# Exponentials and a power on GpSimd, an earlier table load and another recorded order in an S5 scan with a gated MLP

## The chip, the cores and the metric

The kernel runs on one core of a Trainium2 chip. The metric is device time in microseconds of one launch, the median of three runs; lower is better. Engines are written as in the profile: PE (TensorE), DVE (VectorE), ACT (ScalarE), POOL (GpSimd) and SP (SyncE, which here only issues transfers).

## The reference, cut to what matters

The input x has 2048 positions of 448 channels. It is normalized, and the normalized xn goes two ways: through a diagonal complex recurrence with 448 states (an S5 layer), and through a second normalization and an MLP with 1792 hidden units. The result is x + s * silu(m).

```
xn = layernorm(x)                                   # x: 2048 x 448
dt = exp(log_dt); Lam_bar = exp(dt * Lam)
B_bar = ((Lam_bar - 1) / Lam)[:, None] * Bmat
h_t = Lam_bar * h_(t-1) + B_bar @ xn_t              # 448 complex states
s = 2 * real(Cmat @ h_t) + xn * Dskip
m = gelu(layernorm(xn) @ w1 + b1) @ w2 + b2
out = x + s * silu(m)
```

Only exp(dt * Re Lam) is needed as an exponential beside dt itself; the angles go through sines.

## The kernel before, in words

The 2048 positions are worked on in four groups of 512, each of two blocks of 128 partitions with two positions on a partition. For a group, `ln` normalizes, transfers transpose the result to the layout that PE wants (`xn2T` for the MLP, `xnT` for the scan), `mm1_run` multiplies by w1 (L801), ACT applies GELU out of PSUM (L805), `mm2` multiplies by w2 (L828), and DVE adds b2 to each of its four results (L831), in two PSUM banks (5 and 6) by turns. `bu` multiplies by B (L729), `ssm` runs the scan on DVE, `ym` multiplies by C (L871, L874) and joins the two ways. `m0` makes products of C and B once (L712, L697); they need the seven matrices CQ, which DVE makes from C (L659, L661) and from the factors that `parameters` works out on columns of four numbers.

Group 0 is treated apart. Its two blocks come as separate loads; `first_stats` takes the statistics (L431, L432) and the factor (var + eps)^(-1/2) of the two normalizations in one: on ACT, as Ln and Exp (L434, L435 for block 0, L438, L439 for block 1). `first_apply` scales (L453), PE transposes (L460), and copies bring it back from PSUM (L417). `mm1_run` then works block 0 alone, the last two pairs of hidden units with both blocks, and block 1, over three pairs of PSUM banks; each pair has to be emptied by GELU before it is used again. A product of w1 is split in two phases, and the second needs a copy of a part of w1 (L352).

`parameters` turns rows to columns on PE (L529, L530), copies them (L532), and then forms dt = exp(log_dt) on ACT (L533), the angles (L534 to L540), exp(dt * Re Lam) on ACT (L541), the wrapped angles (L542 to L544, and L552), their absolute values on ACT (L554) and the sines (L545 to L551). The rest of it is some thirty products on columns of four (L561, L564, L573, L592).

`b1_columns` turns the rows of b1, which two transfers on POOL bring (L84), into columns (L602, L603, L605). `dummies` gives PE products without use, between the loads; the first 26 run ahead of the parameters.

The order in which the instructions stand on each engine isn't that of the source. Every operation is recorded as a task with what it reads and writes; a list of task numbers (`ORDER`) is the order of issue, and `SECOND` names the tasks that take the second of two engines given for them (POOL or DVE for `small`, ACT or DVE for copies). Semaphore waits follow from the tasks' reads and writes. A tuple of steps (`STEPS`) sets the order of the source after group 0.

Normalization factors of later groups, and of group 0's first normalization, come from `ln_scale` (L478 to L488): on POOL with a power (L480), on DVE with a Newton iteration, as `SECOND` says.

```
def small(fn, reads=(), writes=(), chain=False):
    kb.either(("pool", fn), ("dve", fn), reads, writes, chain=chain)
...
for k in SECOND:
    self.tasks[k].choose(1)
order = [self.tasks[k] for k in ORDER]
```

Of the kernel before, what the change touches and what calls it, by code (L numbers as in the profile page):

```python
# [10 lines left out]
F32 = dt.float32  # L11
# [148 lines left out]


ORDER = [int(k) for k in """
# [17 lines left out]
""".split()]  # L180
SECOND = [int(k) for k in """
45 53 54 61 63 66 69 74 76 83 112 130 133 158 160 162 163 165 177 184 185 187 189 190 220 222 224 226 228 230 238 248 249 258 266 268 331 362 364 365
384 400 401 436 447 468 480 482 487 491 499 501 502 504 510 528 529 609 612 627
""".split()]


# [14 lines left out]
def bass_recurrent_scan__ssm_conv_s5__mixer_channel_mlp__prompt_kernel(  # L201
# [18 lines left out]
    with ExitStack() as es:  # L220
# [2 lines left out]

        ident = SB("ident", [128, 128])
        mhalf = SB("mhalf", [128, 1, 1], F32)
        dk = SB("dk", [128, 3, NK + 2], F32)
        iota = dk[:, 0, 0:NK]
        sgn = SB("sgn", [128, 4], F32)
# [76 lines left out]
        with nc.Block():  # L305
# [18 lines left out]
            pool(lambda e: e.memset(M0[:, 3, :], 0.0), [], ["M0p"], 0.3, S0 + 1)  # L324
            pool(lambda e: e.memset(h_sb[:, :, :, 0:2], 0.0), [], ["hp0", "hp1"], 0.2, S0 + 1)
            pool(lambda e: e.memset(mhalf[:], -0.5), [], ["mhalf"], 0.1, S0 + 1)
            pool(lambda e: e.memset(eps[:, 0:1], LN_EPS), [], ["eps"], 0.1, S0)
            pool(lambda e: e.memset(eps[:, 1:2], LN_EPS * LN_EPS), ["eps"], ["eps"], 0.1, S0)

# [94 lines left out]
            def first_stats(b):  # L424

                for par in range(2):
                    q = 2 * par + b
                    var, mean = lnmv[:, 0, q, 1:2], lnmv[:, 0, q, 0:1]
                    r1, key = lnw[:, 0, 2, 1, q:q + 1], xk(0)[par:par + 1] if b == 0 else xk(1)
                    src, dst = x_all[:, b, par, :], xn2_sb[:, b, par * 512:par * 512 + D]  # L430
                    dve(lambda e, q=q, src=src: e.bn_stats(lnst[:, q, :], src), key, [f"st{q}"])  # L431
                    dve(lambda e, q=q: e.bn_aggr(lnmv[:, 0, q, :], lnst[:, q, :]), [f"st{q}"], [f"mv0_{q}"])  # L432
                    if b == 0:
                        kb.add("act", [lambda e, var=var, r1=r1: e.activation(r1, var, ACT.Ln, scale=1.0 + LN_EPS, bias=eps[:, 1:2]),  # L434
                                       lambda e, r1=r1: e.activation(r1, r1, ACT.Exp, scale=-0.5)], [f"mv0_{q}", "eps", "warm"], [f"r1{q}"], chain=True)  # L435
                    elif par == 1:
                        vs2, rs2 = lnmv[:, 0, 1:4:2, 1], lnw[:, 0, 2, 1, 1:4:2]
                        kb.add("act", [lambda e: e.activation(rs2, vs2, ACT.Ln, scale=1.0 + LN_EPS, bias=eps[:, 1:2]),  # L438
                                       lambda e: e.activation(rs2, rs2, ACT.Exp, scale=-0.5)], ["mv0_1", "mv0_3", "eps", "warm"], ["r11", "r13"], chain=True)  # L439

            def gelu_table():
                kb._sem("gelu0")
                kb.add("act", lambda e: e.preload_act_table_set("gelu_apprx_tanh_and_others"), ["cr", "r10", "r12"] + ["r11", "r13"] * (not 0), ["Wg0"], sem="gelu0")

            def first_apply(b):

# [81 lines left out]
            def parameters():  # L528
# [1 line left out]
                   + [lambda e, i=i: e.matmul(psum[64 * i:64 * i + 64, 7, 12:15], vrows[0:3, 448:512], ident[0:3, 0:3], start=True, stop=True) for i in range(2)],  # L530
                   ["vr0", "vr1", "vr2", "ident"], ["ps7"])
                act(lambda e: e.activation(cw[:, 0:3, :], psum[:, 7, 0:16].rearrange("p (t v) -> p v t", v=4)[:, 0:3, :], ACT.Copy), ["ps7"], ["cp"])  # L532
                act(lambda e: e.activation(col(DT), col(LDT), ACT.Exp), ["cp", "warm"], ["cdt"], 0.2, 3 * PINNED - 4, "exp")  # L533
                small(lambda e: e.tensor_scalar(col(F2), col(LIM), 1.0 / TWO_PI, None, op0=ALU.mult), ["cp"], ["f2"])  # L534
                YA, YB, YC, YD = (ang[:, k, :, :, :] for k in range(4))
                A2 = 2 * PINNED
# [1 line left out]
                small(lambda e: e.tensor_scalar(col(F2), ang[:, 0, 0, 0, :], 2.0, None, op0=ALU.mult), ["f1"], ["f2"])  # L538
                small(lambda e: e.tensor_scalar(ang[:, 0, 0, 1, :], ang[:, 0, 0, 0, :], 512.0, None, op0=ALU.mult), ["f1"], ["f3"])
                small(lambda e: e.tensor_tensor(col(A1), col(DT), col(LRE), ALU.mult), ["cdt", "cp"], ["ca"])  # L540
                act(lambda e: e.activation(col(R1), col(A1), ACT.Exp), ["ca"], ["cr"], 0.2, 3 * PINNED - 1, "exp")  # L541
                wrap = [(lambda e: e.tensor_scalar(YB, YA, ROUND, None, op0=ALU.add)),  # L542
                        (lambda e: e.tensor_scalar(YB, YB, ROUND, None, op0=ALU.subtract)),
                        (lambda e: e.tensor_tensor(YA, YA, YB, ALU.subtract))]  # L544
# [366 lines left out]
            def pr(k, g, x=0.0):  # L911
                return P[k] + 10 * g + x

            dummies(26)
            parameters()
            dummies(8, ["vr0"])
            first_stats(0)
# [103 lines left out]
```

## Time and profile before

| | |
|---|---|
| median of three runs | 153.26 us (153.21 to 153.65) |
| profiled execution, span from first to last instruction | 151.8 us |
| the median less the span | 1.5 us |
| PE busy | 147.1 us, 97% |
| DVE busy | 127.6 us, 84% |
| ACT busy | 99.0 us, 65% |
| POOL busy | 42.1 us, 28% |
| granted TensorE clock, mean | 1.000 |

The profile states the profiled execution's time as its span; what lies around the span is known only as the difference to the median. In the page, a busy PE is not a PE at its peak: products overlap, and their ends are modelled. A row of the timeline gives start, length, engine, line, operation, what is written and read, and in brackets the idle time before it with what ended it. The chain that ended last is followed back from the last instruction; its shares show where a stage hangs, and idle time of an engine that isn't in it costs nothing.

### The profile page before, as it was taken

The page shows a single profiled execution, that of the slowest core. Times are in us where ns is not written, and L with a number is a line of the kernel's source. Part 1 is how long each engine was busy: PE and PEld are TensorE (multiplying, and loading weights), DVE is VectorE, ACT ScalarE, POOL GpSimd, SP SyncE. Part 2 cuts the span into 40 slices and gives each one's busy share as a digit, 9 for nine tenths or more (in the row PEclk, how much of TensorE's full clock was granted, in tenths as well). Part 3 has the DMA queues.
Part 4 walks back from the last instruction along what each step waited for, and adds up shares of the span by engine and source line. Part 5 has one row for each costly group of instructions (what it writes and reads, how often), then busy time and mean ns, then how long its engine had stood idle before and what let it go on. Part 6 is the DMA issues. An engine that isn't in the chain of part 4 may idle for free.

```text
span 151.8 us, 2974 instructions
## 1 busy us (share of the span) xinstructions
PE 147.1 (97%) x1127; PEld 86.6 (57%) x1127; DVE 127.6 (84%) x267; ACT 99.0 (65%) x183; POOL 42.1 (28%) x101
## 2 busy tenths in 40 slices
PE   7899999999999999999999999999999999999992
PEld 7785755454566577545444556764454666555551
DVE  2874999999978979999999996379968726999984
ACT  3888996988789559997898610463579834067400
POOL 5376827153020920010456006200072031000201
PEclk9999999999999999999999999999999999999999
DMA  4999999989997300700003032610331001100022
GB/s 116 262 305 390 266 202 138 219 152 133 165 261 180 65 0 0 138 0 4 0 0 63 4 60 45 154 60 4 60 101 23 0 4 57 64 0 0 4 84 98
DMA packets 31236, 14.73 MB, mean 97 GB/s; under 512 B 24752, under 2 KB 30774, under 8 KB 31222
## 3 DMA queue, kind: packets, MB, share of 16 engines
q1 hardware_dynamic: 30912, 14.26, 41.8%
q0 software_dynamic: 160, 0.23, 1.0%
q8 instruction: 9, 0.15, 0.4%
q10 hardware_dynamic: 150, 0.05, 0.1%
q14 instruction: 5, 0.04, 0.1%
HBM read 6.89 MB, written 1.84 MB: 57 GB/s over the span
## 4 chain that ended last, share of the span: by engine, by line
PE 80%; DVE 9%; DMA 4%; SPq 4%; issue 2%
PE psum L828 23%; PE psum L801 22%; PE psum L729 14%; PE psum L871 13%; DMA x_all<-in_A_x_dram 4%; PE psum L874 4%; SPq L84 4%; PE psum L712 3%; DVE xn_sb L499 2%; DVE lnst L399 1%; DVE s_w L628 1%; PE psum L877 1%; DVE o L831 1%; PE psum L697 1%; DVE tmp L891 1%
## 5 line engine op out<-in xcount | busy, mean ns | idle before, releaser
L801 PE MATMUL psum<-xn2T,w_sb 64*128 64x512 bf16 (+1 forms) x462 | 44.6, 345 | 0.3 <-ACT xn2T L417 0.2
L828 PE MATMUL psum<-w_sb,gT 128*128 128x448 bf16 x224 | 44.5, 353 | 0.2 <-DVE o L831 0.2
L805 ACT ACTIVATE gT<-psum,b1f 128x512 bf16<-128x512 f32 (+1 forms) x66 | 35.9, 625 | 10.4 <-PE psum L801 10.2
L801 PEld LDWEIGHTS psum<-xn2T,w_sb 64*128 64x128 bf16 x462 | 24.1, 109 | 19.8 <-ACT gT L805 2.3
L828 PEld LDWEIGHTS psum<-w_sb,gT 128*128 128x128 bf16 x224 | 21.5, 98 | 20.7 <-DVE o L831 0.6
L417 ACT ACTIVATE u_sb<-psum 128x512 bf16<-128x512 f32 (+2 forms) x22 | 10.5, 478 | 23.0 <-PE psum L729 22.7
L729 PE MATMUL psum<-xnT,BT 128*128 128x256 bf16 x196 | 24.0, 273 | 0.0
L729 PEld LDWEIGHTS psum<-xnT,BT 128*128 128x128 bf16 x196 | 18.9, 98 | 5.4 <-issue 1.1
L891 POOL TENSOR_TENSOR tmp<-t,x_all 128x448 bf16<-128x448 bf16 x5 | 5.2, 1032 | 33.1 <-DVE t L888 30.7
L753 DVE TENSOR_TENSOR_SCAN s_w<-dk,vs 128x774 f32<-128x774 f32 x8 | 14.0, 1760 | 0.1
L500 ACT ACTIVATE xn_sb<-x_all,lnw 128x448 bf16<-128x448 bf16 (+2 forms) x21 | 13.0, 662 | 1.2 <-DVE xn_sb L499 1.1
L417 ACT ACTIVATE vs<-s_w 64x256 bf16<-64x256 f32 (+2 forms) x16 | 10.9, 681 | 2.6 <-DVE s_w L753 1.5
L871 PE MATMUL psum<-CZ,h_sb 128*128 128x448 bf16 x56 | 11.9, 352 | 0.0
L871 PE MATMUL psum<-CQ,h_sb 128*128 128x448 bf16 (+2 forms) x54 | 10.5, 332 | 0.0
L399 DVE BATCH_NORM_STATS2 lnst<-x_all 128x6 f32<-128x448 bf16 x12 | 7.1, 617 | 3.4 <-DMA x_all<-in_A_x_dram 3.4
L831 DVE TENSOR_TENSOR o<-psum,b2bc 128x448 f32<-128x448 f32 x16 | 9.7, 614 | 0.2
L871 PEld LDWEIGHTS psum<-CZ,h_sb 128*128 128x128 bf16 x56 | 5.4, 98 | 4.7 <-DVE lnmv L405 0.4
L871 PEld LDWEIGHTS psum<-CQ,h_sb 128*128 128x128 bf16 x54 | 5.1, 98 | 4.0 <-DVE t L885 0.4
L874 PE MATMUL psum<-M,xnT 128*128 128x448 bf16 x32 | 7.4, 352 | 0.0
L480 POOL TENSOR_TENSOR lnw<-lnw,mhalf 128x8 f32<-128x8 f32 x3 | 7.2, 2404 | 0.3
L883 DVE TENSOR_TENSOR Cr<-psum,xd 128x448 f32<-128x448 f32 x7 | 4.3, 620 | 3.5 <-PE psum L877 3.4
L499 DVE TENSOR_SCALAR xn_sb<-x_all,lnw 128x448 bf16<-128x448 bf16 (+2 forms) x19 | 6.9, 396 | 0.0
(160 smaller groups left out, 189.1 us busy)
## 6 DMA issues: line engine op xcount, KB each, us to landing
out_dram<-tmp SPq DMA_DIRECT2D x7, 224.0 KB, 2.0
x_all<-in_A_x_dram SPq DMA_DIRECT2D x3, 448.0 KB, 4.0
w_sb<-in_B_w_dram SPq DMA_DIRECT2D x3, 448.0 KB, 8.4
w_sb<-in_B_w_dram SPq DMA_DIRECT2D x3, 384.0 KB, 4.8
vs<-in_A_C_re_dram SPq DMA_DIRECT2D x1, 392.0 KB, 11.6
Bn<-in_A_B_im_dram SPq DMA_DIRECT2D x1, 336.0 KB, 10.2
Bn<-in_A_B_re_dram SPq DMA_DIRECT2D x1, 336.0 KB, 10.5
vs<-in_A_C_im_dram SPq DMA_DIRECT2D x1, 336.0 KB, 10.8
```

The source lines that it names most:

```text
L399: dve([lambda e, b=b, par=par, q=q: e.bn_stats(lnst[:, q, :], x_all[:, 2 * g + b, par, :])], [f"x{2 * g + b}"] , [f"st{q}"], 0.62, prio)
L417: kb.either(("act", [lambda e, o=o, i=i: e.activation(o, i, ACT.Copy) for o, i in pairs]), ("dve", [lambda e, o=o, i=i: e.tensor_copy(o, i ...
L499: on = [("dve", [lambda e, o=o, i=i: e.tensor_scalar(o, i, rs, nb, op0=ALU.mult, op1=ALU.add) for o, i in parts], 0.4, 0.12), ("act", [lam ...
L500: ("act", [lambda e, o=o, i=i: e.activation(o, i, ACT.Identity, bias=nb, scale=rs) for o, i in parts], 0.75, 0.2)]
L729: fns = [lambda e, r=r, m=m, d=d: e.matmul(psum[:, 4, r * NK:(r + 1) * NK], BT[:, m, d, :], xnT[:, gx, d, :], start=(d == 0), stop=(d == 6 ...
L753: dve(lambda e, so=so, vi=vi: e.tensor_tensor_scan(so, dk[:].rearrange("p i c -> p (i c)"), vi, 0.0, ALU.mult, ALU.add), ["v", "vl", "dk", ...
L801: return lambda e: e.matmul(view(bk[k]), w1_sb[rows, d, fcol(2 * j + k)], rhs[rows, d, :, :], start=not second and n == 0, stop=second and ...
L805: act([lambda e, k=k: e.activation(gT[:, gb, 2 * j + k, :].rearrange("p (r c) -> p r c", r=2)[:, :, cols], view(bk[k]), ACT.Gelu_apprx_tan ...
L828: fns = [lambda e, fi=fi: e.matmul(psum[:, bk, 0:D], gT[:, gb, fi, q * 128:(q + 1) * 128], w2_sb[:, fi, :], start=(fi == 0), stop=(fi == N ...
L831: dve(lambda e: e.tensor_tensor(o2[:, fb, :], psum[:, bk, 0:D], b2bc[:], ALU.add), [f"ps{bk}", "b2bc"], [f"oo{fb}"], 0.62, prio - 76)
L871: fns = [lambda e, k=k: e.matmul(psum[:, bk, c0:c1], h_sb[:, hb, k, k0:k0 + 128], cm[:, k, c0:c1], start=(k == 0), stop=False) for k in ra ...
L874: fns += [lambda e, d=d: e.matmul(psum[:, bk, c0:c1], xnT[:, gx, d, xs], M0[:, d, c0:c1], start=False, stop=(d == 3)) for d in range(4)]
```

## The change

Block 1's factor of the first group no longer uses ACT: the scaled variance is a `small` operation, and POOL raises it to the power of -1/2. Both exponentials of `parameters` become powers of e on POOL, with a column `euler` that holds e. The load of GELU's table no longer waits for block 1's factors and for the second exponential, only for block 0's factors. There are 30 first dummies in place of 26. `ORDER` and `SECOND` are new lists.

```diff
+        euler = SB("euler", [128, 1], F32)
...
+            pool(lambda e: e.memset(euler[:], math.e), [], ["euler"])
...
                     elif par == 1:
-                        vs2, rs2 = lnmv[:, 0, 1:4:2, 1], lnw[:, 0, 2, 1, 1:4:2]
-                        kb.add("act", [lambda e: e.activation(rs2, vs2, ACT.Ln, scale=1.0 + LN_EPS, bias=eps[:, 1:2]),
-                                       lambda e: e.activation(rs2, rs2, ACT.Exp, scale=-0.5)], ["mv0_1", "mv0_3", "eps", "warm"], ["r11", "r13"], chain=True)
+                        vs2, ws2, rs2 = lnmv[:, 0, 1:4:2, 1], lnw[:, 0, 1, 1, 1:4:2], lnw[:, 0, 2, 1, 1:4:2]
+                        small(lambda e: e.tensor_scalar(ws2, vs2, 1.0 + LN_EPS, LN_EPS * LN_EPS, op0=ALU.mult, op1=ALU.add), ["mv0_1", "mv0_3"], ["w11"])
+                        pool(lambda e: e.tensor_tensor(rs2, ws2, mhalf[:, 0, :].to_broadcast([128, 2]), ALU.pow), ["w11", "mhalf"], ["r11", "r13"])
...
-                kb.add("act", lambda e: e.preload_act_table_set("gelu_apprx_tanh_and_others"), ["cr", "r10", "r12"] + ["r11", "r13"] * (not 0), ["Wg0"], sem="gelu0")
+                kb.add("act", lambda e: e.preload_act_table_set("gelu_apprx_tanh_and_others"), ["r10", "r12"], ["Wg0"], sem="gelu0")
...
-                act(lambda e: e.activation(col(DT), col(LDT), ACT.Exp), ["cp", "warm"], ["cdt"], 0.2, 3 * PINNED - 4, "exp")
+                pool(lambda e: e.tensor_tensor(col(DT), euler[:].to_broadcast([128, 4]), col(LDT), ALU.pow), ["cp", "euler"], ["cdt"])
...
-                act(lambda e: e.activation(col(R1), col(A1), ACT.Exp), ["ca"], ["cr"], 0.2, 3 * PINNED - 1, "exp")
+                pool(lambda e: e.tensor_tensor(col(R1), euler[:].to_broadcast([128, 4]), col(A1), ALU.pow), ["ca", "euler"], ["cr"])
...
-            dummies(26)
+            dummies(30)
```

What the new lists move on the engines, as far as it matters here (lines of the kernel before):

- POOL: the second load of b1 stands behind the sgn memset and select (L311, L312), the ident select and the iota (L315); the loads of b2 and Dskip stand behind the sines and some products of `parameters`.
- PE: the six products of `b1_columns` and the last five dummies stand ahead of the first L801; the first six products of w2 stand among the last L801 of group 0; the first L712 stands behind the first 14 L729.
- ACT: the absolute value (L554) stands ahead of the first GELU; one of block 1's two copies stands among the GELUs; four scaled copies for CQ (L658) stand among the GELUs of the second group.
- DVE: `ln_scale` of group 0 is DVE's, with L478 ahead of the second group's statistics (L399); some twenty operations of `parameters` that were POOL's are DVE's, and they, the copy into dk (L646), and all of the second group's L499 for the MLP stand ahead of the first L831; DVE adds b2 first for the product in bank 6.
- SP: the four transposes of C (Cr) stand ahead of the two of xn for the scan.

More of the change, by code (lines that the diff above doesn't have):

```diff
@@ L162 @@
 ORDER = [int(k) for k in """
[17 rows of a table removed]
[17 rows of a table added]
 """.split()]
 SECOND = [int(k) for k in """
-45 53 54 61 63 66 69 74 76 83 112 130 133 158 160 162 163 165 177 184 185 187 189 190 220 222 224 226 228 230 238 248 249 258 266 268 331 362 364 365
-384 400 401 436 447 468 480 482 487 491 499 501 502 504 510 528 529 609 612 627
+46 54 56 59 64 65 66 67 70 71 72 73 76 77 78 80 81 82 83 84 85 86 87 89 90 102 114 135 157 158 161 162 163 164 165 166 186 187 188 189 190 194 200 222
+226 228 230 236 240 250 251 260 271 355 356 364 366 381 399 400 402 405 446 448 449 451 470 471 501 504 506 509 510 530 532 533 574 607 614 621 633
 """.split()]
```

34 rows, old and new, of the table ORDER are left out of this document.

## The prediction

> **What bounds the kernel now.** I read the page first, then busy time by stage, then the chain that ended last, then the timeline of the first 30 us.
>
> ```profile
> span 151.8 us, 2974 instructions
> ```
>
> The sum below is made against this span of 151.8; the median of the runs, 153.26, lies 1.5 above it, and I leave that 1.5 as it is. A measurement of this kernel can tell about 0.3% (0.46 us) from no change.
>
> Busy time by stage (length of the stage, then busy time and count for each engine):
>
> ```profile
> core 0: us, PE busy (x) PEld busy (x) DVE busy (x) ACT busy (x) POOL busy (x), PEclk, DMA share, GB/s
> 6.85:19.03 12.18, 12.05 (x176) 8.90 (x177) 8.89 (x32) 11.03 (x26) 8.73 (x26) 1.00 1.07 315
> 19.03:30.08 11.05, 10.87 (x58) 5.32 (x58) 10.74 (x33) 9.60 (x17) 3.93 (x13) 1.00 1.14 189
> 30.08:67.57 37.49, 37.49 (x282) 22.39 (x282) 34.46 (x75) 30.57 (x56) 8.71 (x21) 1.00 0.59 112
> 67.57:148.35 80.78, 80.78 (x554) 44.95 (x554) 68.32 (x115) 43.92 (x78) 16.69 (x24) 1.00 0.16 39
> ```
>
> From 30.08 to 148.35 PE never rests: another order can win almost nothing there, it can only lose. What can be won lies before 30. From 19.03 to 30.08 DVE is busy 10.74 of 11.05: beside PE, it is the full engine there.
>
> The chain that ended last (start, length):
>
> ```profile
> 30.15 10.04 PE psum L801 x90
> ...
> 41.83 0.99 PE psum L801 x8
> ...
> 48.62 1.32 PE psum L712 x7
> ...
> 105.72 10.78 PE psum L801 x98
> ```
>
> 98 full-width products of L801 cost 10.78 when nothing holds them. The first group's L801 (70 and 28, partly at half width and twice as many) is the same work.
>
> **Part by part: the head.** From the timeline (start, length, engine, line; in brackets the wait):
>
> ```profile
> 0.83 2.93 PE L422 MATMUL psum<-const-bfloat16-1.0 128*128 128x128 bf16 x26 [0.83 <-PEq L1006]
> ...
> 2.33 0.54 POOL L84 DMA_DIRECT2D dk<-in_B_b_dram  x1
> ...
> 4.03 0.21 PE L529 MATMUL psum<-ident,dk 3*128 3x3 bf16 x3 [0.27 <-DMA dk<-in_A_Lambda_re_dram]
> ...
> 5.63 0.34 POOL L315 IOTA dk<- 128x256 f32 x1
> ...
> 6.34 0.27 PE L602 MATMUL psum<-ident,dk 4*128 4x3 bf16 x4 [0.15 <-DMA dk<-in_B_b_dram]
> 6.48 0.18 PE L603 MATMUL psum<-ident,dk 4*128 4x1 bf16 x2
> 6.85 2.50 PE L801 MATMUL psum<-xn2T,w_sb 64*128 64x256 bf16 x42 [0.19 <-ACT xn2T L417]
> ...
> 9.28 0.62 PE L460 MATMUL psum<-ident,xn_sb 128*128 128x128 bf16 x8
> ...
> 12.64 0.19 POOL L312 TENSOR_SCALAR_AFFINE_SELECT sgn<-sgn 128x1 f32<-128x1 f32 x1
> ```
>
> Four more dummies at 2.93/26 = 0.11 us are 0.45; they fit the stretch from 3.76 to 4.03, where PE waits for a DMA, but for 0.2 at most, and the parameters have that to spare: nothing. Of the memset of e nobody waits.
>
> The searched order moves the second load of b1 on POOL behind the sgn select (0.19), the iota (0.34) and a memset (about 0.1): issued 0.6 later. PE waits for this very load at 6.34, and the new order puts its six products (L602, L603) and five dummies ahead of the first L801. Bounds: 0 late (the transfer lands 3.3 after its issue is over, so some of it may hide) to 0.6 late; I take 0.3. L801 then starts at 6.34 + 0.3 + 0.16 + 5 x 0.08 (L460: 0.62/8) = 7.2 instead of 6.85.
>
> ```profile
> 5.45 1.25 ACT L417 ACTIVATE xn2T<-psum 128x512 bf16<-128x512 bf16 x2
> ...
> 6.90 0.43 DVE L352 COPY w_sb<-w_sb 64x512 bf16<-64x512 bf16 x2
> ...
> 7.29 1.28 ACT L443 ACT_TABLE_LOAD   x1
> ...
> 8.67 2.30 ACT L805 ACTIVATE gT<-psum,b1f 128x256 bf16<-128x256 f32 x6
> ...
> 9.54 0.62 DVE L624 TENSOR_SCALAR s_w<-dk,cw 128x256 f32<-128x256 f32 x2
> ...
> 12.74 0.23 ACT L554 ACTIVATE ang<-ang 128x16 f32<-128x16 f32 x1
> ```
>
> ACT loses block 1's Ln and Exp and both exponentials of the parameters, so GELU's table starts behind the copies, at 6.75, and is there at 8.03 instead of 8.57. But the order now puts the Abs of the angles (0.23, at 12.74 before) ahead of all GELUs. It waits for DVE's wrap, which stands behind the copy of b1 (its product ends at 6.66 + 0.3, so 7.0). From there DVE has two L624 (0.6), two copies of w1 (0.4) and six small operations, the wrap's three one after the other (0.65 by L561 below): 1.65, so Abs at 8.65 and the first GELU at 8.8 or 8.9, not earlier than 8.67. The table's gain is given back. The Trainium skill (ScalarE: Activation LUTs, "What ACT_TABLE_LOAD costs") gives 1283 ns and about 1380 ns of drain for a switch of sets; the trace disagrees on the drain, since the first GELU starts 0.1 behind the load. By the page the first GELU would come at 9.4, and the first rival's time would be 0.5 higher.
>
> The powers: the nearest row is the same operation on 8 columns.
>
> ```profile
> L480 POOL TENSOR_TENSOR lnw<-lnw,mhalf x3: 1897/2261/3053, 9.3 to 78.2; 128x8 f32<-128x8 f32 x3
> ```
>
> ```profile
> 5.42 0.26 POOL L540 TENSOR_TENSOR cw<-cw 128x4 f32<-128x4 f32 x1 [2.55 <-ACT cw L533]
> ```
>
> Bounds for one on 4 or 2 columns: 0.26 (a plain product) and 1.9 to 3.05. By column, (1.9 - 0.2)/8 = 0.21, so 1.05 and 0.6; I take these. The parameters' products end near 4.4, so dt's power starts at 4.7 and ends at 5.75; four small operations at 0.3 follow, block 1's power runs 7.4 to 8.0, and DVE reaches block 1's apply at 8.8. So it is covered by 0.8; without that cover each us costs PE one.
>
> Stage 6.85 to 19.03: without waits it is 10.78 + 0.62 = 11.4; 12.18 were used, so 0.8 of waits on GELU and copies. The new one starts 0.35 late and keeps 0.2 of waits: 7.2 + 11.4 + 0.2 = 18.8, that is -0.2 (bounds -0.8 and +0.4).
>
> **The second product of w2.** This is what I count on.
>
> ```profile
> 13.58 2.21 DVE L399 BATCH_NORM_STATS2 lnst<-x_all 128x6 f32<-128x448 bf16 x4 [1.95 <-DMA x_all<-in_A_x_dram]
> ...
> 17.65 0.16 DVE L478 TENSOR_SCALAR lnw<-lnmv 128x4 f32<-128x4 f32 x1
> ...
> 19.03 8.12 PE L828 MATMUL psum<-w_sb,gT 128*128 128x448 bf16 x42
> ...
> 19.92 0.17 DVE L488 SCALAR_TENSOR_TENSOR lnw<-lnmv,lnw 128x8 f32<-128x8 f32 x1
> ...
> 22.07 0.15 DVE L561 TENSOR_TENSOR cw<-cw,ang 128x4 f32<-128x4 f32 x1
> ...
> 22.77 0.62 DVE L831 TENSOR_TENSOR o<-psum,b2bc 128x448 f32<-128x448 f32 x1
> ...
> 27.33 2.82 PE L828 MATMUL psum<-w_sb,gT 128*128 128x448 bf16 x14 [0.18 <-DVE o L831]
> ```
>
> ```profile
> 32.94 3.58 ACT L805 ACTIVATE gT<-psum,b1f 128x512 bf16<-128x512 f32 x6
> ...
> 36.98 0.68 DVE L646 COPY dk<-cw 128x768 f32<-128x768 f32 x1
> ```
>
> ```profile
> b2bc<-in_B_b_dram POOLq DMA_DIRECT2D x1, 112.0 KB, 7.0
> ```
>
> ```profile
> L628 DVE SCALAR_TENSOR_TENSOR s_w<-dk,cw,s_w 128x256 f32<-128x256 f32 x2 | 0.9, 466 | 0.0
> L626 DVE TENSOR_SCALAR s_w<-s_w 128x1024 f32<-128x1024 f32 x1 | 0.7, 694 | 0.0
> ```
>
> The products alternate between two PSUM banks, so the third needs the first bank's addition (L831) done. Before, DVE took 9.19 from the landing of x (13.58) to that addition (22.77), and the third product began at 19.03 + 28 x 0.193 = 24.4, a cover of one us. In the new order the stretch from the same statistics to the addition has 22 operations on 4 columns more (0.1 alone, 0.2 where one feeds the next, 0.15 long by L561's row: 2.5), the copy into dk (0.6) and one more L628 (0.4); it lacks L626 and one table row, done earlier (0.9). That is 9.2 + 2.6 = 11.8. The first scale factors (2.3, by L478 to L488), POOL's before, fill DVE's wait for x, so DVE still starts near 13.7. The addition starts at 25.5 and ends at 26.1; PE, which asks at 24.1, starts the third product at 26.2. Two products of 2.7 later the second group's L801 starts at 31.6 instead of 30.15: **+1.4** (bounds +0.6 and +2.2, for 0.8 on the count). b2, which that addition reads too, is now issued by POOL behind the sines, near 15.6; 7.0 later, at 22.6, it is still in time.
>
> **The first product of C and B.** L712 stood at 48.62; it is moved ahead of 8 L801, 14 L729, 14 L828 and 14 L729 (0.99 + 1.64 + 2.65 + 1.53 = 6.8). All seven CQ must be ready by 31.6 + 10.8 + 1.6 = 44.0. From 25.5 DVE has some 18 us to do until then, the last of them at 43.9, and three hang on copies that ACT now runs between the GELUs. Bounds 0 and 0.8; I take 0.2. On SP the four transposes of C go ahead of two of x; the first that PE wants is due at 42, nothing. The tail's last addition is 256 wide instead of 192: 0.
>
> Sum: +1.4 + 0.2 = +1.6 on a stage end that carries the head with it: 153.26 + 1.6 = **154.9**.
>
> **The rivals.** *DVE is in time* (faster): if the addition starts before 23.4, that is if the small operations cost their 0.08 of issue and no more, the third product isn't held; then the head's 0.2 to 0.8 and the 0.3 that PE lost around 27.33 are won, together 0.8: 152.4. For it: they lie beside long ones; against it: 10.74 of 11.05. Chance 0.20. *Gain and loss cancel*, half of that lateness: 153.3, 0.07.
>
> *CQ is late*: ACT's scaled copies stand behind GELUs that began 2.8 after L801 (32.94 to 30.15), so at 34.4; five pairs of 1.2 (3.58/3) bring it to 40.4, the copies among them past 43, and CQ6 can miss 44 by a us: 156.0, chance 0.16. *A power costs per call*: 1.9 each, so block 1's ends at 9.75 rather than 8.0 and DVE, PE's transposes and all behind them slip by 0.95: 155.9, chance 0.12. The Trainium skill (GPSIMD Engine Reference, "Key points") says that GpSimd shares its SBUF interfaces with VectorE and contends with its two-port and two-input instructions; the spread 1897 to 3053 agrees, and by it this rival would cost up to 3 us. *The forecast*: 0.45.
>
> The range takes in most of the first rival and all of the second: 152.1 to 156.7. Faster 0.20, same 0.07, slower 0.45 + 0.16 + 0.12 = 0.73.
>
> **What would show it.** Right: the first L801 near 7.2; first GELU at 8.7 to 9.2 behind Abs; PE waiting over one us for DVE's addition near 25; the second group's L801 from 31 on; the products of B and C within a us behind their bu. Wrong: the addition before 23.4, or a power that takes the head with it.

## The result, and the profile after

| | before | after |
|---|---|---|
| median of four runs each | 153.37 us (153.21 to 153.65) | 155.12 us (154.67 to 155.87) |
| ratio, 95% interval | | 1.0119 (1.0089 to 1.0149) |
| profiled execution, its time and span | 153.26, 151.8 | 155.87, 154.1 |
| mean granted TensorE clock of it | 1.000 | 0.989 |

The changed kernel is 1.2% slower: 1.75 us by the medians, where 1.6 had been forecast. The profiled execution is the longest of the four, and it has something that two of the others have not: a TensorE clock below 1. The page of the changed kernel, busy times and the clock in 40 slices of 3.85 us:

```profile
span 154.1 us, 2992 instructions
PE 148.7 (96%) x1131; PEld 88.1 (57%) x1131; DVE 128.3 (83%) x301; ACT 99.7 (65%) x184; POOL 29.5 (19%) x72
PEclk9969999999999999999999999999999999999999
```

The third slice grants 6 tenths. Two stretches by stage (length, busy time and count of PE, weight loads, DVE, ACT, POOL, then the clock) show where the half clock lies:

```profile
3.85:7.27 3.42, 2.57 (x36) 1.78 (x33) 3.21 (x15) 2.79 (x8) 2.72 (x10) 1.00 0.95 267
7.27:10.68 3.41, 3.37 (x32) 2.89 (x34) 3.22 (x15) 1.85 (x4) 3.03 (x8) 0.50 1.02 332
```

And the timeline of the changed kernel, engine by engine:

```profile
4.74 1.05 POOL L535 TENSOR_TENSOR cw<-euler,cw 128x4 f32<-128x4 f32 x1 [0.26 <-ACT cw L534]
7.17 0.73 POOL L441 TENSOR_TENSOR lnw<-lnw,mhalf 128x2 f32<-128x2 f32 x1
...
6.78 1.28 ACT L445 ACT_TABLE_LOAD   x1
8.76 0.22 ACT L556 ACTIVATE ang<-ang 128x16 f32<-128x16 f32 x1 [0.69 <-DVE ang L546]
9.74 0.84 ACT L807 ACTIVATE gT<-psum,b1f 128x256 bf16<-128x256 f32 x2 [0.76 <-PE psum L803]
...
25.06 0.62 DVE L833 TENSOR_TENSOR o<-psum,b2bc 128x448 f32<-128x448 f32 x1
...
5.73 0.40 PE L462 MATMUL psum<-ident,xn_sb 128*128 128x128 bf16 x4 [0.43 <-DVE xn_sb L455]
6.44 0.27 PE L604 MATMUL psum<-ident,dk 4*128 4x3 bf16 x4 [0.31 <-DMA dk<-in_B_b_dram]
7.31 4.10 PE L803 MATMUL psum<-xn2T,w_sb 64*128 64x256 bf16 x42
...
21.81 9.63 PE L830 MATMUL psum<-w_sb,gT 128*128 128x448 bf16 x50
31.38 2.98 PE L803 MATMUL psum<-xn2T,w_sb 64*128 64x512 bf16 x26
36.96 5.63 PE L803 MATMUL psum<-xn2T,w_sb 64*128 64x512 bf16 x50 [0.23 <-ACT gT L807]
```

Read quickly, this looks like the forecast come true: the second group's L803 starts at 31.38, and 31.6 was predicted. It is not. The 50 products of w2 run through from 21.81 without a wait for DVE. What is late is their start, for two reasons: six products of w2 already ran ahead of them (18.92 to 20.16), which is the same work in another place, and the first 42 L803 took 4.10 at half clock instead of 2.50. The wait that the prediction counted on isn't in this trace at all. The runs of the same kernel at clock 1.000 took 154.67 and 155.00, still 1.3 to 1.6 above before. So two questions: what the half clock is worth, and where the loss lies without it.

### The profile page after: what moved, and what is told of

The parts are those of the page before. It is cut to its first block, busy times and chain, and to the rows that moved or that the text cites. A ratio compares the mean times of both kernels' runs of the same rounds, so it can differ in the third digit from the quotient of the medians.

```text
span 154.1 us, 2992 instructions
## 1 busy us (share of the span) xinstructions
PE 148.7 (96%) x1131; PEld 88.1 (57%) x1131; DVE 128.3 (83%) x301; ACT 99.7 (65%) x184; POOL 29.5 (19%) x72
## 4 chain that ended last, share of the span: by engine, by line
PE 70%; ACT 21%; DMA 4%; issue 2%; POOL 1%; DVE 1%; POOLq 0%; ACTq 0%
PE psum L803 21%; PE psum L830 17%; PE psum L873 13%; PE psum L731 11%; ACT gT L807 7%; ACT xn_sb L502 5%; PE psum L876 4%; ACT WT L642 2%; DMA dk<-in_B_b_dram 2%; DMA xn2T<-xn_sb 2%; PE psum L714 2%; ACT u_sb L419 2%; ACT g_sb L835 1%; PE psum L879 1%; ACT L620 1%
## 5 line engine op out<-in xcount | busy, mean ns | idle before, releaser
L803 PE MATMUL psum<-xn2T,w_sb 64*128 64x512 bf16 (+1 forms) x462 | 45.9, 355 | 0.4 <-ACT gT L807 0.2
L803 PEld LDWEIGHTS psum<-xn2T,w_sb 64*128 64x128 bf16 x462 | 25.5, 111 | 20.0 <-ACT gT L807 2.6
L731 PE MATMUL psum<-xnT,BT 128*128 128x256 bf16 x196 | 24.0, 273 | 0.1
L419 ACT ACTIVATE u_sb<-psum 128x512 bf16<-128x512 f32 (+2 forms) x23 | 11.1, 481 | 17.5 <-PE psum L731 17.3
L731 PEld LDWEIGHTS psum<-xnT,BT 128*128 128x128 bf16 x196 | 19.0, 98 | 5.5 <-issue 0.8
L502 ACT ACTIVATE xn_sb<-x_all,lnw 128x448 bf16<-128x448 bf16 (+2 forms) x23 | 13.8, 656 | 4.2 <-DVE xn_sb L501 2.4
L893 POOL TENSOR_TENSOR tmp<-t,x_all 128x448 bf16<-128x448 bf16 x4 | 4.5, 1126 | 40.3 <-DVE t L887 21.1
L419 ACT ACTIVATE vs<-s_w 64x256 bf16<-64x256 f32 (+2 forms) x12 | 8.2, 683 | 1.8 <-DVE s_w L755 1.1
L837 ACT ACTIVATE th<-o 128x448 f32<-128x448 f32 x8 | 4.6, 575 | 6.4 <-DVE o L833 6.4
L660 ACT ACTIVATE tmp<-Cr,cw 128x448 f32<-128x448 bf16 (+1 forms) x10 | 6.6, 675 | 0.6 <-DVE CZ L663 0.6
L835 ACT ACTIVATE g_sb<-o 128x448 bf16<-128x448 f32 x8 | 4.4, 569 | 3.8 <-DVE o L833 3.8
```

The lines of the kernel that those rows point to most:

```text
L419: kb.either(("act", [lambda e, o=o, i=i: e.activation(o, i, ACT.Copy) for o, i in pairs]), ("dve", [lambda e, o=o, i=i: e.tensor_copy(o, i ...
L502: ("act", [lambda e, o=o, i=i: e.activation(o, i, ACT.Identity, bias=nb, scale=rs) for o, i in parts], 0.75, 0.2)]
L660: on = [("act", [lambda e, o=o, i=i, c=c: e.activation(tmp[o, k, :], b[i], ACT.Copy, scale=c[i]) for o, i, c in ps], 0.66 * len(ps), 0.2), ...
L731: fns = [lambda e, r=r, m=m, d=d: e.matmul(psum[:, 4, r * NK:(r + 1) * NK], BT[:, m, d, :], xnT[:, gx, d, :], start=(d == 0), stop=(d == 6 ...
L803: return lambda e: e.matmul(view(bk[k]), w1_sb[rows, d, fcol(2 * j + k)], rhs[rows, d, :, :], start=not second and n == 0, stop=second and ...
```

## The experiments

Each is an edit of the changed kernel's list of issue, or of the list of an earlier experiment that its text names, unless it says otherwise; the rows of the diffs are instructions of one engine in their order. "Ratio" is to the kernel before on the same chip in the same session. It is not the quotient of the two medians, and differs from it by up to 0.4% (1.0041 and 1.0081 in d1_before_bunched).

### The dummies back between the transposes

```diff
 PE: L462 x4
+    L424 x3
     L462 x4
+    L424 x2
     L604 x4, L605 x2
-    L424 x5
     L803 x42
```

> The three and the two dummy products of L424 stand again between and behind the two transposes of block 0, as before; all else is the changed kernel. In the profile of the changed kernel the TensorE clock is at half from 7.27 to 10.68 and the first 42 L803 take 4.10 instead of 2.50. Theory A (the prediction's): the clock is no part of the loss; with it full the 42 L803 take 2.5 again, but PE then stands before DVE's addition (L833) near 24 for 0.7 to 1.4, the second group's L803 starts at 30.6 to 31.4, and the time is 1.2 to 1.6 above before. Theory B (the clock): the bunched dummies cost nearly all; with the clock full PE isn't held near 24, the second group's L803 starts at 30.0 to 30.3, and the time is within 0.4 of before.

Measured: 155.06 us (154.76 to 155.79) beside 153.60 before, ratio 1.0073 (1.0042 to 1.0104); clock 1.000 in the profile, and 0.996 or more in all eleven executions. Timeline of this kernel:

```profile
6.96 2.72 PE L803 MATMUL psum<-xn2T,w_sb 64*128 64x256 bf16 x42 [0.21 <-ACT xn2T L419]
24.88 5.46 PE L830 MATMUL psum<-w_sb,gT 128*128 128x448 bf16 x28 [0.38 <-DVE o L833]
30.27 5.36 PE L803 MATMUL psum<-xn2T,w_sb 64*128 64x512 bf16 x48
35.86 5.63 PE L803 MATMUL psum<-xn2T,w_sb 64*128 64x512 bf16 x50 [0.23 <-ACT gT L807]
...
64.71 0.94 PE L731 MATMUL psum<-xnT,BT 128*128 128x256 bf16 x7 [0.29 <-ACT u_sb L419]
...
149.59 0.27 PE L879 MATMUL psum<-CQ,h_sb 128*128 128x256 bf16 x1
...
8.77 0.22 ACT L556 ACTIVATE ang<-ang 128x16 f32<-128x16 f32 x1 [0.65 <-DVE ang L546]
8.89 2.28 ACT L807 ACTIVATE gT<-psum,b1f 128x256 bf16<-128x256 f32 x6
...
14.57 0.62 DVE L401 BATCH_NORM_STATS2 lnst<-x_all 128x6 f32<-128x448 bf16 x1
24.11 0.62 DVE L833 TENSOR_TENSOR o<-psum,b2bc 128x448 f32<-128x448 f32 x1
```

PE's last product of the kernel before:

```profile
148.66 0.25 PE L877 MATMUL psum<-CQ,h_sb 128*128 128x192 bf16 x1
```

Theory B falls: with a full clock the median is still 1.46 above that of the kernel before (1.75 in the changed kernel; the intervals overlap). What the half clock adds to an execution is 0.9 by the two profiles (spans of 154.1 and 153.2). Theory A is right that DVE's addition now holds PE, but the wait is 0.38, and the second group starts only 0.2 later than before (30.27 to 30.08). The span, 153.2, is 1.4 longer than before. So 1.2 us are lost *behind* 30, where the prediction expected almost nothing. From 30.27 to the end of PE's last product, 149.86, are 119.6; before it was 30.08 to 148.91, 118.8. From there to the end of the span are 3.3 instead of 2.9. The account of the spans is 0.2 + 0.75 + 0.45 = 1.4.

### The first additions of b2 earlier

```diff
 DVE: L501 x2, L630, L501 x2 (second group), L648 (copy into dk)
+     L833 (bank 6)
      L594, L563, L501 x5
-     L833 (bank 6)
+     L833 (bank 5)
      L661, L663, L661, L600   (L661: the first of Bn)
-     L833 (bank 5)
```

> As e1_dummies_back, and DVE makes the first addition of b2 (for bank 6) right behind the copy into dk, ahead of the last three of the second group's scalings, and the second addition ahead of the first L661; before the addition for bank 6 stood behind them. Theory A: the wait of PE near 24 goes, the second group's L803 starts at 29.9 to 30.3, and of the time 0.6 to 1.2 is won against e1_dummies_back. Theory C (the gain is taken back): the second group's L803 starts as early, but PE then waits as long for the first product of C and B (L714), whose CQ DVE makes no earlier; the time stays within 0.3 of e1_dummies_back. Theory B: the same as e1_dummies_back within 0.3, with no wait in either.

Measured: 155.05 us (154.72 to 156.59) beside 153.60 before, ratio 1.0101 (1.0065 to 1.0136): nothing gained.

```profile
29.74 4.71 PE L803 MATMUL psum<-xn2T,w_sb 64*128 64x512 bf16 x42
34.79 0.84 PE L803 MATMUL psum<-xn2T,w_sb 64*128 64x512 bf16 x6 [0.34 <-ACT gT L807]
35.95 5.64 PE L803 MATMUL psum<-xn2T,w_sb 64*128 64x512 bf16 x50 [0.32 <-ACT gT L807]
...
30.47 0.61 DVE L833 TENSOR_TENSOR o<-psum,b2bc 128x448 f32<-128x448 f32 x1
...
32.09 1.28 ACT L620 ACT_TABLE_LOAD   x1 [0.39 <-ACT g_sb L835]
```

The wait at 24 is gone and the group starts 0.53 earlier, but PE then stands 0.66 for GELU. Theory C named the right outcome and the wrong place. GELU's table is loaded behind the fourth g (L835), which needs DVE's fourth addition; that came at 30.47, 0.7 behind PE's product. The load itself starts 0.39 behind L835 here, as in the changed kernel and all others with its order near 30, and 0.08 behind it in the kernel before and in e3_code_old_order; why was not found.

### The new code with the old order

```diff
-ORDER, SECOND of the changed kernel
+ORDER, SECOND of the kernel before, renumbered; the powers on POOL
+ahead of what needs them, the scaled variance (L440) on DVE
```

> The changed code (both exponentials and block 1's power on POOL, the early table, 30 dummies) with the order and the choices of the kernel before; the power of exp(dt Re Lam) stands right ahead of the sines, block 1's power behind the first angle, its scaled variance on DVE. Theory A: the code costs nothing and the new order all of it; the first GELU starts at 8.2 to 8.6 since no Abs stands ahead of it, PE waits for nothing between 23 and 30, and the time is 0 to 0.8 below before. Rival (a power costs its cover, as POOL has 1.05, 0.7 and 1.15 more to do in the old order ahead of the angles, the factors and the sines): block 1's transposes start 0.4 or more later than 9.28, or L628 and the second group's factors slip, and the time is 0.5 to 1.5 above before.

Measured: 153.40 us (153.13 to 155.22) beside 153.60 before, ratio 0.9987 (0.9953 to 1.0022).

```profile
6.74 1.28 ACT L445 ACT_TABLE_LOAD   x1
8.21 0.84 ACT L807 ACTIVATE gT<-psum,b1f 128x256 bf16<-128x256 f32 x2 [0.18 <-PE psum L803]
...
19.04 10.77 PE L830 MATMUL psum<-w_sb,gT 128*128 128x448 bf16 x56
29.74 10.11 PE L803 MATMUL psum<-xn2T,w_sb 64*128 64x512 bf16 x90
```

The code costs nothing that can be told from noise, so the order costs all. The first GELU comes 0.46 earlier than before (8.21 to 8.67), and the first w2 product starts at 19.04, before at 19.03: the earlier table is worth nothing, since PE's own L803 set that stage. The second group starts 0.34 earlier, and PE's wait of 0.18 at 27.33 for DVE is gone.

### The absolute value behind the first GELUs

```diff
 ACT: L445 (table)
-     L556
      L807 x2
+     L556
      L807 x4
```

> As e2_addition_early, and the Abs of the angles (L556) stands on ACT behind the first pair of GELUs rather than ahead of all. Theory A: with a full clock the first GELU starts at 8.3 to 8.6 instead of 8.9 to 9.1, the table's gain is there, the stage of w1 in group 0 ends 0.2 to 0.5 earlier, and the time follows by 0 to 0.4 as DVE is no bound in it. Rival: the first GELU is held by PE's products or by b1's copy rather than by the Abs; nothing moves by more than 0.1.

Measured: 155.83 us (154.85 to 156.12) beside 153.60 before, ratio 1.0111 (1.0067 to 1.0156), which is that of e2_addition_early within the noise. The first GELU starts 1.42 behind the first L803 (8.83 and 7.41) instead of 1.99 (8.90 and 6.91 in e2_addition_early), and then it waits 0.26 for PE's products. From the first L803 to the last 50 products of w2 are 13.2 and 13.3. GELU was earlier against PE, and PE gained nothing by it; the rival is right on the time. The whole trace is 0.4 later here; the clock was full only from 6.5 on (in e2_addition_early from 4.0).

### New head and old rest, and the reverse

```diff
 h1: ORDER of e1_dummies_back up to the second group's first L803,
     then the old order of all that is left
 h2: the old order up to there, then the new order of all that is left
```

> The changed code; the order of the changed kernel (with the dummies of L424 between and behind the transposes, as in e1_dummies_back) up to the second group's first L803, and from there the order of the kernel before for whatever is left. In e1_dummies_back PE waited 0.38 for DVE's addition, the second group's L803 started at 30.27 against 30.08 before, and the span was 1.4 longer. Theory A (the prediction's: the loss is made ahead of 30 and carried to the end): 1.0 to 1.5 above before. Theory D (the head costs 0.2, the rest is lost one by one behind it, and 0.45 of it in the last transfers): 0 to 0.4 above before, and from PE's last product to the end of the span 2.8 to 2.9 as before.

> The complement of h1_new_head_old_rest: the changed code, the order of the kernel before up to the second group's first L803, and from there the order of the changed kernel (31 small operations and copies, which the changed order has ahead of that point and the other has not, come first). Theory A: within 0.4 of before, since the wait of PE near 24 isn't there. Theory D: 0.9 to 1.6 above before: 0.45 from PE's last product to the end of the span (3.3 instead of 2.9), 0.3 near 64 where PE waits behind L699, 0.2 where the last group's L803 is split, and what DVE and ACT are late with CQ.

Measured: h1 154.52 us (154.43 to 154.59) beside 153.68 before, ratio 1.0030 (0.9988 to 1.0072), in between the theories: its second group starts at 30.47 and PE waits there for GELU again (0.21). The third group starts 0.96 later than in the kernel before (68.53 and 67.57) and the last product ends 0.97 later, so the new head passes its lateness on into the second group, and behind that the old order loses nothing; from the last product to the end are 2.96. h2 took 158.35 (157.27 to 158.97), ratio 1.0266 (1.0215 to 1.0317), and tells nothing of either theory, since the seam made a wait of its own:

```profile
36.81 0.84 PE L803 MATMUL psum<-xn2T,w_sb 64*128 64x512 bf16 x6 [2.42 <-ACT gT L807]
```

### The last transfers

```diff
 SP:  output of 224 KB (last group, block 0)   <- here
      output of 112 KB (last group, block 1)
-     output of 224 KB
      output of 64 KB
```

> As e1_dummies_back, and on SP the 224 KB output of the last group's first block is issued ahead of the 112 KB one of the second, as in the kernel before; there it stood behind it and was issued at 150.27, 1.4 after its data were there, beside the last two. Theory D: from PE's last product to the end of the span 2.85 to 3.0 instead of 3.34, and the time 0.35 to 0.5 below e1_dummies_back. Theory A (the tail costs nothing, as the prediction has it): within 0.2 of e1_dummies_back.

Measured: 154.44 us (154.35 to 154.83) beside 153.68 before, ratio 1.0030 (0.9988 to 1.0072); against e1_dummies_back 0.6 by the medians of two sessions, 0.5 by the spans (152.7 and 153.2). SP's issues, e1_dummies_back first:

```profile
149.88 1.32 SPq L84 DMA_DIRECT2D out_dram<-tmp  x3
```

```profile
148.87 2.17 SPq L84 DMA_DIRECT2D out_dram<-tmp  x3
```

From PE's last product to the end 2.9 instead of 3.3, as Theory D has it. It was not the width of the last addition: DVE is done 0.9 behind PE either way. What differs is that the last 64 KB take 2.0 from issue to landing in e1_dummies_back, where the 224 KB move beside them, and 1.6 here. The same stretch is 3.3 in the changed kernel and in each with its transfers, and 2.8 to 3.0 in those with the earlier issue. The exception is r1_old_order_from_50 below with 3.24: there the 224 KB were issued early too, and the last 64 KB took 2.1. So the earlier issue won 0.4 of the 0.45 here; that the 224 KB beside them are the whole reason is not shown.

### The kernel before with the dummies bunched

```diff
 PE (before): L460 x4
-             L422 x3
              L460 x4
-             L422 x2
              L602 x4, L603 x2
+             L422 x5
              L801 x42
```

> The kernel before with one edit: its three and two dummies of L422 stand behind b1's products, ahead of the first L801, as in the changed kernel, not between and behind the transposes. Theory of the clock (a stretch of 3.4 in which PE is busy 2.6 or less brings the clock to half for the next 3.4): at least some executions show a mean clock of 0.985 to 0.997, and take 0.5 to 1.7 longer than those at 1.000; the median is 0.2 to 1.5 above before. Rival: the changed order's half clock came from its other moves; every execution has a clock of 1.000 and the time is within 0.3 of before.

Measured: 154.92 us (153.77 to 156.46) beside 153.68 before, ratio 1.0041 (0.9980 to 1.0102). Two of its six executions have a clock of 0.989 and took 155.3 and 156.0; the four at 0.998 or more took 153.8, 153.8, 154.5 and 156.5, the longest of all. The profiled one has 0.989:

```profile
5.22:8.63 3.41, 1.86 (x29) 1.37 (x27) 2.79 (x12) 2.49 (x7) 1.45 (x7) 1.00 1.00 266
8.63:12.04 3.41, 3.41 (x36) 3.03 (x31) 1.24 (x5) 1.43 (x3) 2.55 (x5) 0.50 1.04 309
```

```profile
6.32 0.40 PE L460 MATMUL psum<-ident,xn_sb 128*128 128x128 bf16 x4 [0.91 <-DVE xn_sb L453]
...
7.09 0.28 PE L602 MATMUL psum<-ident,dk 4*128 4x3 bf16 x4 [0.38 <-DMA dk<-in_B_b_dram]
```

So the half clock comes without the new order too. That the bunching alone brings it is not shown. In this execution the second transposes and b1's products were also 0.65 and 0.75 later than in the kernel before (5.67 and 6.34), for waits that the edit doesn't touch; and the kernel before has a clock of 0.989 in 6 of 66 executions, e3_code_old_order in one of 12. For the bunching speaks the count: 3 of 10 executions of the two kernels that have it, and none of 67 of the nine kernels that have the new head with the dummies between the transposes. The median's interval holds no change.

### The old order from 50 on; the second group freed; both

```diff
 r1: e1_dummies_back up to the second L714, then the old order
 g2: e2_addition_early, transfers as in t1_transfer_earlier;
 DVE: L663 x2
+     L833 (third)
      L661, L376
+     L833 (fourth)
      L663, L850, ...
-     L612 x3 ahead of CQ's last L663, now behind it
 gr: g2 up to the second L714, then the old order
```

> As e1_dummies_back up to the second L714 (near 50), and from there the order of the kernel before for what is left. Theory D, from e1_dummies_back's profile against that of before: behind 50 it loses 0.36 at L699 near 64, 0.16 ahead of the third group's L803, 0.1 to 0.2 where the last group's L803 is split, and 0.45 in the last transfers, 1.0 in all; so the time is 0.8 to 1.1 below e1_dummies_back, and 0.3 to 0.7 above before. Theory A (all is lost ahead of 30): within 0.2 of e1_dummies_back, 1.2 to 1.6 above before.

> As e2_addition_early with the output's transfer of t1_transfer_earlier, and on DVE the third addition of b2 ahead of L661, the fourth ahead of the next L663, and three small L612 behind the last L663 for CQ. In e2_addition_early what was won at 30 was lost again to GELU: PE stood 0.66 in the second group's L803, as the fourth addition came 0.7 behind PE and GELU's table is loaded behind it. Theory E (ACT's table, behind DVE's late fourth addition, holds the second group): PE stands 0.2 or less in that L803, the L731 start at 40.6 to 41.0 instead of 41.5, and unless CQ is late the time is 0.3 to 0.8 below t1_transfer_earlier, 0 to 0.6 above before. Theory C (CQ takes it): the L731 start as early, but L714 waits for L663, and the time is within 0.2 of t1_transfer_earlier.

> g2_second_group_freed up to the second L714 and from there the order of the kernel before, as in r1_old_order_from_50: all named losses are taken away. Theory D with E: the time is that of e3_code_old_order, 0.2 below to 0.3 above before. If a loss is missing in the list: 0.5 or more above before.

Measured: r1 155.56 us (155.37 to 155.85), ratio 1.0130 (1.0082 to 1.0178); gr 155.62 (155.48 to 158.01), ratio 1.0132 (1.0085 to 1.0180). Both miss their expectations and leave the question open, since again the seam between the lists made a wait; in r1_old_order_from_50:

```profile
51.43 0.93 PE L731 MATMUL psum<-xnT,BT 128*128 128x256 bf16 x7 [0.99 <-ACT u_sb L419]
```

In gr_all_freed it is 1.52. g2_second_group_freed took 155.16 us (154.33 to 156.08) beside 153.36 before, ratio 1.0108 (1.0055 to 1.0161), in the profile:

```profile
35.42 5.63 PE L803 MATMUL psum<-xn2T,w_sb 64*128 64x512 bf16 x50 [0.21 <-ACT gT L807]
43.01 1.50 PE L714 MATMUL psum<-CQ,Bn 128*128 128x448 bf16 x7 [0.32 <-DVE CQ L663]
```

PE's wait for GELU is back to 0.21, L731 starts at 41.0 (41.5 in e2_addition_early), and then L714 waits for CQ: that is Theory C in the trace. In time neither theory is met: the median is 0.7 above that of t1_transfer_earlier in another session, the span 0.3 (153.0 and 152.7). Two repairs in a row, e2_addition_early and this one, each uncovered the next wait: for the addition, for GELU, for CQ. That suggests that the three are one.

### The columns back on POOL

```diff
-SECOND: DVE for L563, L566, L594 to L600 (23 operations)
+POOL for these; b2 and Dskip issued ahead of them;
+the additions of b2 (L833) where DVE reaches them as their products end
```

> As g2_second_group_freed, but 23 of the small operations of the parameters on columns (L563, L566, L594 to L600), which the changed kernel has on DVE, stand on POOL, as most of them did in the kernel before; the loads of b2 and Dskip are issued ahead of them, and the four additions of b2 stand where DVE's shorter list reaches them as their products end. Theory F (DVE's work until the last CQ is the bound, and the waits for b2's addition, for GELU and for CQ are three faces of it): DVE's last L663 for CQ ends near 41.5 instead of 42.9, PE waits for neither the first addition nor CQ, and the time is 0.3 to 0.6 below g2_second_group_freed, 0.3 to 0.9 above before. Rival (POOL takes four times as long for each, and CQ's factors come too late, or ACT with its six more operations is the bound): PE waits for CQ or GELU as long as before, and the time is within 0.2 of g2_second_group_freed or above.

Measured: 154.22 us (154.06 to 155.69) beside 153.47 before, ratio 1.0054 (1.0024 to 1.0084). PE's rows, of which only that for GELU has a wait, and DVE's first addition and last L663 for CQ:

```profile
29.61 5.36 PE L803 MATMUL psum<-xn2T,w_sb 64*128 64x512 bf16 x48
35.18 5.63 PE L803 MATMUL psum<-xn2T,w_sb 64*128 64x512 bf16 x50 [0.21 <-ACT gT L807]
...
42.28 1.49 PE L714 MATMUL psum<-CQ,Bn 128*128 128x448 bf16 x7
...
67.76 9.96 PE L803 MATMUL psum<-xn2T,w_sb 64*128 64x512 bf16 x90
...
22.97 0.62 DVE L833 TENSOR_TENSOR o<-psum,b2bc 128x448 f32<-128x448 f32 x1 [0.17 <-PE psum L830]
...
41.30 0.69 DVE L663 SCALAR_TENSOR_TENSOR CQ<-Cr,cw,tmp 128x448 bf16<-128x448 bf16 x1
```

DVE now waits for PE, not PE for DVE; CQ is done at 42.0 (43.0 in g2), and L714 starts right behind its predecessor. The same stretch in three kernels, before, e1_dummies_back and this one:

```profile
14.57:42.66 28.09, 27.78 (x234) 14.77 (x230) 26.56 (x73) 24.04 (x41) 11.05 (x35) 1.00 1.05 192
```

```profile
14.57:42.66 28.09, 27.48 (x238) 15.18 (x233) 26.95 (x89) 26.88 (x47) 2.90 (x10) 1.00 0.90 173
```

```profile
14.57:42.66 28.09, 27.88 (x241) 15.55 (x236) 25.82 (x71) 27.32 (x47) 6.32 (x31) 1.00 1.00 189
```

In this stretch the new order takes 8 us from POOL, for which the other engines waited 0.2 in all, and gives 16 operations to DVE, which was nearly full, and six to ACT; at the same time it has CQ wanted 5.5 us earlier (first L714 at 42.96 instead of 48.46). DVE is busy 26.95 of 28.09, little more than the 26.56 before; so it is late mostly because its work is due earlier. Theory F holds for the addition and for CQ, though CQ is done at 42.0 and not near 41.5; it doesn't hold for GELU, for which PE waits 0.21 as in g2_second_group_freed. The time is 0.94 below that kernel by the medians of two sessions and 0.7 by the spans (152.3 and 153.0), where 0.3 to 0.6 was expected, and 0.75 above before, as expected. The experiment moves the columns, the loads and the additions at once, so it doesn't say what each of them is worth.

What is left, 0.75 by the medians and 0.5 by the spans, wasn't undone alone. In this trace the second group starts 0.47 earlier than before (29.61), but the third only 0.19 later than before (67.76 and 67.57): 0.66 is lost between them. Of the 0.75 in e1_dummies_back's trace 0.47 is lost there too, most of it in the wait of 0.29 at 64.71 and the switches between kinds of products around it (L699 between two L731 rather than ahead of L828: about 0.4 in all). Another 0.17 lies between the third group's first L803 and the product behind its 90 (10.04, before 9.87), and 0.1 where the last group's L803 is in two pieces, 3.20 for 28 and 7.79 for 70, where 98 in one took 10.85. That these are the rest is argued from the traces, not shown.

## Why the prediction was right, and where it was not

The time was right (154.9 forecast, 155.12 measured), and so was the direction, but that the total agrees is luck: one term was 1.2 too large, and losses of about 1.2 had hardly a term. The account was mostly wrong. Step by step:

- *PE never rests from 30 on; another order can only lose there.* Right, and it should have been taken seriously: 0.75 were lost there, and the sum had 0.2 for it.
- *Four more dummies.* Nothing, as said. That the other five move was counted as 0.4 of work ahead of L801 and nothing else; the half clock of the profiled execution (0.9 of its span, against e1_dummies_back) had no term.
- *Second load of b1*: issued 0.7 later, landed 0.1 later (6.31 to 6.20). Taken was 0.3 of bounds 0 to 0.6.
- *GELU's table*: load 6.78 (6.75 forecast), Abs 8.77 (8.65), first GELU 8.89 at full clock (8.8 to 8.9). By the Trainium skill (ScalarE: Activation LUTs, "What ACT_TABLE_LOAD costs") a drain of 1380 ns would have put it at 9.4; at 6.74 + 1.28 the next ACT operation came 0.19 later in e3_code_old_order, and that one waited for PE. The step that "the table's gain is given back" by the Abs is right on the times and wrong on the reason: without the Abs in front there was no gain either.
- *Powers*: by column. 1.05, 0.73 and 1.15 measured for 4, 2 and 4 columns, 1.05 and 0.6 forecast; *a power costs per call* falls. (Its own price was too low: two powers of 1.9 end 2.15 later, at 10.15, not at 9.75.) Whether DVE's traffic is behind the spread of the powers on 8 columns was not tested. Block 1's ends at 8.10 in e1_dummies_back and DVE's apply starts at 8.92: covered by 0.8, as said.
- *Stage of w1*: forecast an end of 18.8; in e1_dummies_back 20.17 less six products of w2 in 1.24, so 18.9.
- *The second product of w2* is the step that failed. The addition was forecast for 25.5 and came at 24.11; PE's wait was to move the second group by 1.4, and the wait was 0.38. The count of DVE's stretch was wrong: from the statistics to the addition 9.54 (14.57 to 24.11) against 9.19 before, so +0.35 and not +2.6. The 22 operations on columns cost about 0.07 each where they don't feed one another, and were taken at 0.1 to 0.2; and seven of them stand ahead of the statistics. With these seven the first factors fill more than the wait for x, so DVE began 0.9 later than assumed; with a start at 13.7 it would have ended the addition at 23.9, ahead of PE, which asked at 24.5.
- *CQ*: forecast +0.2, and without another change 0 (L714 at 42.96 right behind L731). It became 0.32 as soon as the waits ahead of it were taken away. The 6.8 by which L712 was said to move counts eight L801 that still stand ahead of it; it moved by 5.5. *CQ is late* was the right place for the wrong amount.
- *DVE is in time*, the faster rival: e2_addition_early has its condition, an addition before 23.4 (23.10), and not its gain; it took as long as e1_dummies_back, since GELU holds PE next.
- *The tail*: 0 forecast, 0.45 measured. Looked at was the width of the last addition; what counted was SP's queue, where a transfer of 224 KB was put behind one of 112 KB.

So by the profiles +1.4 and +0.2 stood for 0.2 in the head, 0.75 spread behind it and 0.45 in the last transfers. The engine was right (DVE, filled with what POOL had done), the place was not.

## What to carry to other kernels

A total that agrees doesn't confirm its terms: compare the time of the same product in both traces at four or five places, and see where the gap opens. If taking away one wait uncovers the next of the same engine, count what that engine has to do up to the last of them, instead of repairing waits. And when a list of issue changes, read the queue of the transfers at the very end too, since nothing hides what is issued there.

## What the runs showed of the hardware

The clock can go to half without a long pause. In the changed kernel the stretch of 3.42 with PE busy 2.57 is followed by 3.41 at half clock, and its longest pause is 0.43; in the kernel before with bunched dummies PE was busy 1.86 of 3.41, in h2_old_head_new_rest 0.87 around the wait of 2.42. The first stretches at full clock of eleven kernels, with 2.68 to 3.06 of 3.41, were followed by the full clock. But the busy share, by the profile's modelled ends, does not decide alone: counted in steps of 3.41 from where the clock became full (5.15), r1_old_order_from_50 has one around its wait of 0.99 with less than 2.57, and the full clock follows it. Its row, and that of h2_old_head_new_rest, which the half clock follows:

```profile
49.52:52.94 3.42, 2.42 (x20) 1.68 (x18) 3.14 (x7) 2.28 (x5) 2.78 (x5) 1.00 0.55 109
...
34.35:37.76 3.41, 0.87 (x8) 0.26 (x6) 3.29 (x8) 3.02 (x5) 0.00 (x0) 1.00 1.02 131
```

An estimate from the shapes in the timelines: the three stretches that were followed by half speed stream some 3000 to 3400 columns through PE (in two of them many products are 3 or 128 columns wide, in h2_old_head_new_rest there are few), r1's stretch 5300, and the eleven first ones 3900 to 11000. What the clock goes by was not tested. The Trainium skill (TensorE: Matmul & The Clock Gate, "What's actually happening") has the clock fall back after an idle window of about 3.4 us; the length of the window agrees, that it must be idle doesn't. The Trainium skill says there too that the window runs free of the kernel's start: the first full stretch began between 3.6 and 6.5 us in the profiles here, which fits. That would explain why one kernel meets the half clock in some executions and not in others; no run shows it.

The four executions of h2_old_head_new_rest at 0.988 or 0.989 took 158.3 to 159.0, the two at 1.000 157.3 and 157.4. In the kernel before, three at 0.989 took 154.75 to 154.84 in one session, where most took 153.2 to 153.8; but four at 0.998 or more took 154.69 to 154.93 there as well, so the half clock is not the only thing that makes an execution 1.4 us longer. What the other is stayed open.
